# Infini-attention beside a top-1 mixture of experts: the last expert's second product as rows added into the output, and the last gathers, moved into the attention

## The chip, the cores and the metric

One core of a Trainium2 chip. Its engines run in parallel, each in its own order of instructions: TensorE (PE, matrix products), VectorE (DVE), ScalarE (ACT), GpSimd (POOL), and SyncE (SP), which here issues most DMAs; POOL issues the indirect ones. The metric is the device time of one execution in microseconds (us), smaller is better. The tables give the median of several runs and, apart from it, the one execution that the profiler recorded.

## The reference

`x` is 2048 x 512 in float32 (one batch). The output is a sum of three terms:

```
xn  = layernorm(x)
out = x + attention(xn) + moe(xn)

attention: q, k, v = xn@wq, xn@wk, xn@wv      32 heads of 16, four segments of 512 tokens
  per segment s: p = softmax(q k^T/4 + mask); a_dot = p v
                 a_mem = phi(q) M / (phi(q) z + 1e-6);  o = g*a_mem + (1-g)*a_dot
                 M += phi(k)^T v;  z += sum phi(k)          g = sigmoid(beta)
  result: o @ wo
moe: each token goes to the one expert with the largest logit of xn @ w_gate (8 experts)
  softmax over that single logit, so its weight is 1
  result: silu(xn @ w1[e]) @ w2[e]                512 -> 1376 -> 512
```

## The kernel before

**Precision and shapes.** Every float32 product of a weight is made of three float16 products: both operands are split into a high and a low half, and `mm3` (L406 to L409) adds high*high, low*high and high*low in one bank of the accumulator. The splits run on ACT, DVE and POOL (L388, L389 and L395 to L398). PE works in three shapes: full 128 x 128 tiles (projections, experts, `wo`), 64-row tiles (q times k, L1291) and 32-column tiles (probabilities times values, L1410).

**Stages.** The front computes layer norm, the q, k and v projections (their high and low halves are written by L785 and L786 and stored to `Q_d`, `K_d`), the memory terms (L791, L817, L823 to L826) and the routing. The routing sorts the experts by the number of their tokens, gives each rank a capacity (`CAPS`), and writes the lists of token indices by products of a one-hot `yT` (L690) with a table of selected values. The experts follow in that order: rows of `x` gathered (L1071), normalized and turned, the first product (`xgh, xgl` with `wh, wl`), silu (L1165, L1166, split into `hh, hl`), the second product. The second product has the weight tile as the stationary operand, so its result stands with features as partitions and tokens as columns; it is turned (L1175) and stored to the scratch tensor `ye_d` (L1185). Meanwhile the attention runs by units of heads: maxima (L1291 with a reduction on DVE, L1326), scores (L1291) with exp on ACT (L1383), a causal select on POOL (L1387), value products (L1410), normalization, and the output product `wo * oT`.

**The end.** For each of the 16 tiles of 128 tokens a row of `ye_d` is gathered by an indirect DMA on POOL (L1527), weighed on ACT (L1494), added to `x` on DVE (L1544), the output product is added on DVE (L1551), and the tile is stored to `out` (L1554). All 16 gathers need the last expert's rows in `ye_d`; the last tile of the output is made in two halves.

**What sets the order.** All instructions are recorded by a planner: each stage is a generator process with a key, and costs per instruction and due times (`QKV0`, `MOE0`, `ATT0`, `SLOT`, `PVA`, `OUT` and so on at the head of the file) decide which one PE and the other engines take next. On the chip each engine goes through its row of instructions in exactly that order and waits by semaphores for data.

## Time and profile before

| | us |
|---|---|
| median of 3 runs (lowest, highest) | 666.51 (663.81, 666.88) |
| the profiled execution | 669.71 |
| its span from first to last instruction | 667.8 |
| PE busy in the span | 639.8 (96%) |
| DVE, ACT, POOL busy | 546.1 (82%), 485.7 (73%), 383.8 (57%) |
| granted TensorE clock, mean | 0.984 |

The profiled execution lies 3.20 us above the median, and 1.9 us of it lie outside the span. Busy times are shares of the whole span; the rows below show single stretches.

### The profile page before, as it was taken

Reading aid. Unit: us, or ns where it says so; the run is one execution under the profiler, and the core shown is the slowest. Engines: PE = TensorE matmul, PEld = TensorE weight load, DVE = VectorE, ACT = ScalarE, POOL = GpSimd, SP = SyncE. Lnnn points to the kernel's source line nnn. Section 1 sums busy time; section 2 is a strip of 40 time slices with the busy share of each in tenths; the row PEclk is TensorE's granted clock in tenths of the full one; section 3 lists DMA queues with packets and bytes.
Section 4 is the critical chain, followed back from the end, with each engine's and each line's share of the span. In section 5 each row is a group of like instructions: output and inputs, shape, how many; then the busy total and the mean of one; then the engine's idle time right before and its main releaser. Section 6 shows DMA issues by size and latency. Waiting matters only on the chain.

```text
span 667.8 us, 17326 instructions
## 1 busy us (share of the span) xinstructions
PE 639.8 (96%) x5914; PEld 392.6 (59%) x5914; DVE 546.1 (82%) x1801; ACT 485.7 (73%) x1069; POOL 383.8 (57%) x596
## 2 busy tenths in 40 slices
PE   7999999999999899999999999989999999999965
PEld 5555555555675455656565566656566666677522
DVE  6875899844677999999998898999989989995435
ACT  5965475534561597999888688968778898899533
POOL 3510035001264487688768576876858786888770
PEclk9999999999999899999999999989999999999987
DMA  8813667435566557665584476564645666864485
GB/s 287 305 51 104 229 205 243 135 119 193 169 210 214 171 168 193 186 169 156 169 219 120 129 200 168 156 173 135 167 130 159 183 161 187 225 153 104 140 268 206
DMA packets 149054, 117.79 MB, mean 176 GB/s; under 512 B 34170, under 2 KB 136698, under 8 KB 148450
## 3 DMA queue, kind: packets, MB, share of 16 engines
q1 hardware_dynamic: 146290, 108.13, 54.9%
q0 software_dynamic: 2672, 8.52, 4.3%
q8 instruction: 47, 0.77, 0.5%
q14 instruction: 45, 0.37, 0.2%
HBM read 87.32 MB, written 29.30 MB: 175 GB/s over the span
## 4 chain that ended last, share of the span: by engine, by line
PE 71%; DVE 8%; ACT 7%; DMA 7%; issue 3%; another core or an unknown queue 2%; SPq 1%; POOL 1%; DVEq 0%; POOLq 0%; ACTq 0%
PE b L407 17%; PE b L409 15%; PE b L408 15%; PE b L1291 11%; PE b L1410 10%; DVE junk L1326 2%; DMA att<-in_A_x_dram 1%; PE b L817 1%; ACT pt L1383 1%; PE b L1098 1%; DMA K_d<-qkhl 1%; DMA Ks<-K_d 1%; DMA wh<-in_A_wk_dram 1%; DMA Qs<-Q_d 1%
## 5 line engine op out<-in xcount | busy, mean ns | idle before, releaser
L1326 DVE CUSTOM_DVE_ANT_0 junk<-b,mask 128x384 f16<-128x384 f32 (+3 forms) x512 | 218.7, 480 | 10.4 <-PE b L1291 9.3
L1383 ACT ACTIVATE pt<-b 128x512 f32<-128x512 f32 x320 | 173.1, 611 | 26.2 <-PE b L1291 25.8
L398 POOL TENSOR_TENSOR wl<-wst,wh 128x512 f16<-128x512 f32 (+3 forms) x120 | 119.1, 1004 | 50.3 <-ACT wh L396 44.0
L1387 POOL TENSOR_SCALAR_AFFINE_SELECT pt<-pt 128x256 f32<-128x256 f32 x256 | 111.0, 452 | 57.3 <-ACT pt L1383 55.8
L407 PE MATMUL b<-xgh,wh 128*128 128x288 f16 (+9 forms) x352 | 98.3, 279 | 0.9 <-DVE yb L1175 0.6
L407 PE MATMUL b<-hh,wh 128*128 128x288 f16 (+7 forms) x352 | 98.1, 279 | 0.3 <-DVE mxt L1326 0.2
L409 PE MATMUL b<-xgh,wl 128*128 128x288 f16 (+9 forms) x352 | 97.6, 277 | 0.0
L408 PE MATMUL b<-xgl,wh 128*128 128x288 f16 (+9 forms) x352 | 97.5, 277 | 0.0
L408 PE MATMUL b<-hl,wh 128*128 128x288 f16 (+7 forms) x352 | 97.4, 277 | 0.0
L409 PE MATMUL b<-hh,wl 128*128 128x288 f16 (+7 forms) x352 | 97.4, 277 | 0.0
L407 PEld LDWEIGHTS <-wh 128*128 128x128 f16 (+2 forms) x704 | 69.7, 99 | 39.2 <-issue 29.3
L398 POOL TENSOR_TENSOR hl<-yT,hh 128x288 f16<-128x288 f32 (+7 forms) x88 | 64.2, 731 | 36.1 <-ACT hh L396 35.5
L389 DVE SCALAR_TENSOR_TENSOR wl<-wst,wh 128x512 f16<-128x512 f32 (+2 forms) x96 | 74.1, 780 | 5.4 <-ACT wh L388 4.7
L1410 PE MATMUL b<-pt,vau 128*32 128x512 f32 (+3 forms) x1024 | 76.9, 436 | 0.7 <-ACT pt L1383 0.3
L395 ACT ACTIVATE wst<-wst 128x512 f32<-128x512 f32 (+3 forms) x120 | 63.9, 550 | 18.7 <-DVE mxt L1326 17.4
L409 PEld LDWEIGHTS <-wl 128*128 128x128 f16 (+2 forms) x704 | 69.9, 99 | 10.7 <-issue 0.2
L408 PEld LDWEIGHTS <-wh 128*128 128x128 f16 (+2 forms) x704 | 70.1, 100 | 9.9 <-issue 1.1
L1291 PE MATMUL b<-Ks,Qs 64*128 64x384 f16 (+3 forms) x512 | 64.5, 300 | 3.4 <-DVE mxt L1326 2.2
L388 ACT ACTIVATE wh<-wst 128x512 f16<-128x512 f32 (+2 forms) x96 | 54.8, 571 | 12.9 <-DMA wst<-in_B_w_dram 12.7
L396 ACT ACTIVATE wh<-wst 128x512 f16<-128x512 f32 (+3 forms) x120 | 61.4, 551 | 0.2
L1291 PE MATMUL b<-Qs,Ks 64*128 64x384 f16 (+3 forms) x512 | 61.4, 300 | 0.1
L1410 PEld LDWEIGHTS b<-pt,vau 128*32 128x32 f32 x1024 | 30.4, 109 | 46.5 <-issue 35.5
(209 smaller groups left out, 1192.2 us busy)
## 6 DMA issues: line engine op xcount, KB each, us to landing
wst<-in_B_w_dram SPq DMA_DIRECT2D x32, 640.0 KB
wst<-in_B_w_dram SPq DMA_DIRECT2D x24, 768.0 KB
Qs<-Q_d SPq DMA_DIRECT2D x64, 98.0 KB
Ks<-K_d SPq DMA_DIRECT2D x64, 98.0 KB
K_d<-qkhl SPq DMA_DIRECT2D x48, 128.0 KB
Q_d<-qkhl SPq DMA_DIRECT2D x48, 128.0 KB
vau<-V_d SPq DMA_DIRECT2D x16, 304.0 KB
V_d<-va SPq DMA_DIRECT2D x4, 1120.0 KB
```

Source lines behind the costliest of these rows:

```text
L389: yield vec(n, lambda: V.scalar_tensor_tensor(lo, src, scale, hi, op0=ALU.mult, op1=ALU.subtract), two=True)
L395: yield act(n, lambda: A.activation(src, src, AF.Copy, scale=scale), True)
L396: yield act(n, lambda: A.activation(hi, src, AF.Copy), True)
L398: yield gps(pool(n), lambda: G.tensor_sub(lo, src, hi))
L407: PE.matmul(outp, lh, rh, start=start, stop=False)
L408: PE.matmul(outp, lh, rl, start=False, stop=False)
L409: PE.matmul(outp, ll, rh, start=False, stop=stop)
L1291: PE.matmul(bs[a][:, off : off + w], lhs, rhs, start=True, stop=True)
L1326: yield vec(w, lambda: V.tensor_tensor_reduce(out=jk[:, :w], in0=b[:, off : off + w], in1=mask[:, L - w :], op0=ALU.add, op1=ALU.max, scal ...
L1383: yield act(L, lambda: A.activation(dst, src, AF.Exp))
L1387: yield gps(360, lambda: G.affine_select(dg, dg, pattern=[[0, 2], [1, P]], compare_op=ALU.is_ge, fill=0.0, base=0, channel_multiplier=-1))
L1410: PE.matmul(vb[32 * hh : 32 * hh + 32, j * P :], va[:, j, VW * h : VW * h + 32], ptt[u][0][:, hh // 2, hh % 2, POFF[j] : POFF[j] + w], sta ...
```

## The change

- The rank of the experts is changed: the sixth largest becomes the last, with capacity 256 (two row tiles of 128); the two smallest move one place forward.
- The last expert's second product has tokens as the stationary operand: for each of two row tiles, 11 chunks of the hidden dimension, three matmuls of 512 columns each. Its weights are loaded as whole rows of `w2`. All its weight splits stay on DVE (`VLAST`), and so does the low half of its silu (`ELAST`).
- These rows don't go to `ye_d`. When all tiles of `out` are stored, the last expert's rows are gathered from `out` (two indirect DMAs on POOL, L1264), the product is added on DVE (L1273), and they are scattered back (two indirect DMAs on POOL, L1275). For this a list of its tokens and gates (`tokl`, `gatel`) is made at the end of the routing by 16 one-hot tiles (L798) and 32 small products with 3 columns (L802); the planner lets expert 0's first product be recorded after that list.
- The 16 gathers from `ye_d` (now L1640) need seven experts and stand in the midst of the last attention units, in five buffers. The gather is added by four multiply-adds on DVE in place of the ACT pass and one add. Rows of `x` for late tiles go to buffers that are free earlier, each of the last four behind the store of the tile four before it.
- The first tiles of q and k (`Qs0`, `Ks0`) lie in a pool of their own, so that their loads and the first maxima no longer wait for the front's pool to be closed.
- The planner's constants are retuned.

```diff
-CAPS = (288, 288, 288, 270, 256, 256, 240, 224)
+CAPS = (288, 288, 288, 270, 256, 240, 224, 256)
...
+FST, SUMK, VLAST, ELAST = 83625.4532, 590731.4436, 56, 7
...
+        for t in range(NT):
+            rm = T(mp, (P, NL * P), F16, f"yT{t % 3}")
+            yield vec(NL * P, lambda: V.tensor_scalar(rm[:], ri[:, : NL * P], rankl[:, t, :], None, op0=ALU.is_equal))
+
+            def products():
+                for j in range(NL):
+                    PE.matmul(bl[:, j, :3], rm[:, j * P : (j + 1) * P], sell[:, t, :3],
+                              start=t == 0 and j == 0, stop=t == NT - 1 and j == NL - 1)
...
+        yield from chain(lists2)
+        banks.put(n, "M")
+        yield fl.settle()
+        listedl.up()
...
-        if share[0] >= 1.0:
+        if share[0] >= 1.0 and n < VLAST:
...
             yield prepped[e].wait()
+            if e == 0:
+                yield listedl.wait()
...
+            if e == E - 1:
+                iw = yield wst.get()
+                yb = T(mp, (P, 4 * 384), F32, f"wst{iw}")
+                for j in range(NL):
+                    fl.spawn(last_base(j, min(P, cap - j * P), yb[:, j * D : (j + 1) * D]), fl.cur.key + j)
+                for j in range(NL):
...
+                    for f, (fo, fw) in enumerate(FCH):
...
+                        yield pe(3 * 216, lambda: mm3(b[:w], hh[:fw, f, sl], hl[:fw, f, sl], h[:fw, f % 3, :],
+                                                      l[:fw, f % 3, :], f == 0, f == NF - 1))
+                    fl.spawn(last_rows(j, w, n, b, yb[:, j * D : (j + 1) * D]), fl.cur.key)
+                break
...
+    def last_base(j, w, yr):
+
+        yield summed.wait()
+        yield gps(1270, lambda: G.indirect_dma_start(
+            out=yr[:w], out_offset=None, in_=out,
+            in_offset=bass.IndirectOffsetOnAxis(ap=tokl[:w, j : j + 1], axis=0)), fl.software)
...
+    def last_rows(j, w, n, b, yr):
+
+        yield lastly.wait()
+        yield vec(D, lambda: V.scalar_tensor_tensor(yr[:w], b[:w], gatel[:w, j : j + 1], yr[:w], op0=ALU.mult, op1=ALU.add))
+        banks.put(n, "D")
+        yield gps(1100, lambda: G.indirect_dma_start(
+            out=out, out_offset=bass.IndirectOffsetOnAxis(ap=tokl[:w, j : j + 1], axis=0), in_=yr[:w], in_offset=None), SWD)
...
+        for t in range(LATE, NT):
+            i = t - LATE
+            if i < TPS:
+                att[t] = tiles[i]
+            else:
+                yield stored[i - TPS].wait()
...
+        tiles = T(mp, (P, NBLK[0] * P), F32, "yb")
+        tiles = [tiles[:, :D], tiles[:, D : 2 * D], T(mp, (P, D), F32, "yg")[:]]
+        tiles += [T(mp, (P, D), F32, nm)[:] for nm in ("xgn1", "yh")]
+        for t in range(NT):
+            i = yield yts.get()
             yield gps(1270, lambda: G.indirect_dma_start(
-                out=yt, out_offset=None, in_=ye_d[:],
-                in_offset=bass.IndirectOffsetOnAxis(ap=home_i[:, t : t + 1], axis=0)), SWE)
...
+            for q in range(4):
+                V.scalar_tensor_tensor(a[:, :, q, :], y[:, q], gates[:, t : t + 1], a[:, :, q, :], op0=ALU.mult, op1=ALU.add)
```

**The order on POOL near the end.** `pt` are the probabilities of an attention unit. Before, the gathers stand behind the last select:

```order
L398 TENSOR_TENSOR wl3_2201_10489<-wst1_2217_10607,wh3_2200_10488 96x128
L1387 AFFINE_SELECT pt0_2218_10664<-pt0_2218_10664 128x2x128 x7
L1441 TENSOR_TENSOR ot0_2156_10308<-ot0_2156_10308,omt0_2101_10039 128x32x16
L1387 AFFINE_SELECT pt1_2232_10771<-pt1_2232_10771 128x2x128 x8
L1527 DMA wh0_2251_10901<-ye_d_2_67,home_i_30_109 128x512
L1527 DMA wl0_2252_10902<-ye_d_2_67,home_i_30_109 128x512
L1527 DMA wh1_2253_10903<-ye_d_2_67,home_i_30_109 128x512
```

Now the last of the 16 stand between the selects of the last two units, and the new gather and scatter of `out` end the row:

```order
L1640 DMA yb_2223_10540<-ye_d_2_67,home_i_30_109 128x512
L1640 DMA yg_2224_10541<-ye_d_2_67,home_i_30_109 128x512
L1640 DMA xgn1_2225_10542<-ye_d_2_67,home_i_30_109 128x512
L1508 AFFINE_SELECT pt1_2231_10567<-pt1_2231_10567 128x2x128 x7
L1640 DMA yh_2226_10543<-ye_d_2_67,home_i_30_109 128x512
L1508 AFFINE_SELECT pt1_2231_10567<-pt1_2231_10567 128x2x128
L1562 TENSOR_TENSOR ot0_2135_10052<-ot0_2135_10052,omt0_2072_9762 128x32x16
L1640 DMA yb_2223_10540<-ye_d_2_67,home_i_30_109 128x512
L1264 DMA wst0_2268_10888<-out_0_dram,tokl_32_111 128x512 x2
L1275 DMA out_0_dram<-wst0_2268_10888,tokl_32_111 2048x512 x2
```

The gathers have moved ahead of the last selects, which now stand behind them on the same queue.

**The order on PE at expert 0's first product.** `xh, xl` with `whq, wlq` is a projection, `xgh, xgl` is expert 0's first product, `Mst` the memory product. Before, projections stand between pieces of expert 0:

```order
L407 LDWEIGHTS wh0_190_1211
L407 MATMUL b0_391_2440<-xgh_302_1938,wh0_190_1211 128x288
L408 LDWEIGHTS wh0_190_1211
L408 MATMUL b0_391_2440<-xgl_303_1939,wh0_190_1211 128x288
L409 LDWEIGHTS wl0_191_1212
L409 MATMUL b0_391_2440<-xgh_302_1938,wl0_191_1212 128x288
L407 LDWEIGHTS whq_44_129
L407 MATMUL b6_389_2421<-xh0_153_910,whq_44_129 128x512
L408 LDWEIGHTS whq_44_129
L408 MATMUL b6_389_2421<-xl0_154_911,whq_44_129 128x512
L409 LDWEIGHTS wlq_47_132
L409 MATMUL b6_389_2421<-xh0_153_910,wlq_47_132 128x512
```

Now all projections are done when expert 0 begins, and the last products of the list (`yT` one-hot) and of the memory stand directly ahead of it:

```order
L802 LDWEIGHTS yT0_427_2622
L802 MATMUL b4_332_2088<-hl_73_246,yT0_427_2622 128x3
L881 MATMUL b0_429_2627<-Mst3_58_143,phe2_423_2604 128x136 x2
L881 MATMUL b1_431_2647<-Mst3_58_143,phe2_423_2604 128x136 x2
L414 LDWEIGHTS wh0_198_1257
L414 MATMUL b6_435_2653<-xgh_319_2019,wh0_198_1257 128x288
```

Expert 0's first product has moved behind the list and the last memory products, where nothing else stands beside it.

**The order on DVE at the same place.** Before, the last projection's halves (`qkhl`, L786) and `phe` (L791) stand among the silus of expert 0 (`yT`, L1166):

```order
L1166 SCALAR_TENSOR_TENSOR yT2_420_2622<-yT2_420_2622,b6_418_2598 128x288
L786 SCALAR_TENSOR_TENSOR qkhl1_425_2653<-b0_414_2576,qkhl1_425_2653 128x512
L1166 SCALAR_TENSOR_TENSOR yT0_429_2673<-yT0_429_2673,b5_421_2623 128x288
L791 SCALAR_TENSOR_TENSOR phe0_426_2654<-phe0_426_2654,phr1_427_2655 128x512
L1166 SCALAR_TENSOR_TENSOR yT1_431_2692<-yT1_431_2692,b4_428_2672 128x288
L823 TENSOR_TENSOR dn10_434_2708<-b3_433_2695,e6_42_127 128x16
```

Now they stand among the one-hot tiles of the list (L798):

```order
L798 TENSOR_SCALAR yT0_421_2600<-hl_73_246 128x256
L890 TENSOR_TENSOR oms0_411_2554<-b5_418_2588,dn01_419_2591 128x256
L798 TENSOR_SCALAR yT1_425_2610<-hl_73_246 128x256
L798 TENSOR_SCALAR yT2_426_2617<-hl_73_246 128x256
L848 SCALAR_TENSOR_TENSOR qkhl1_422_2603<-b2_408_2532,qkhl1_422_2603 128x512
L798 TENSOR_SCALAR yT0_427_2622<-hl_73_246 128x256
L853 SCALAR_TENSOR_TENSOR phe2_423_2604<-phe2_423_2604,phr1_424_2605 128x512
L381 TENSOR_SCALAR gatel_33_112<-b4_332_2088 128x1
```

The one-hot tile of the list's last product has moved behind the halves of the last projection.

**The order on PE at the end.** Before, PE ends with the two 256-column halves of the output product's last tile:

```order
L408 LDWEIGHTS oTh1_2115_10132
L408 MATMUL b0_2288_11124<-wo_h_27_106,oTh1_2115_10132 128x256
L409 LDWEIGHTS oTl1_2116_10133
L409 MATMUL b0_2288_11124<-wo_h_27_106,oTl1_2116_10133 128x256
L1664 TENSOR_LOAD nb_i_40_120
```

Now it ends with 45 matmuls of the last expert's second product (`hh, hl` with `wh, wl`), behind the output products:

```order
L415 LDWEIGHTS hh_2207_10444
L415 MATMUL b6_2283_11097<-wh3_2274_10958,hh_2207_10444 128x512
L416 LDWEIGHTS hl_2208_10445
L416 MATMUL b6_2283_11097<-wh3_2274_10958,hl_2208_10445 128x512
L1772 TENSOR_LOAD nb_i_42_122
```

Between the last value product and these 45 there are 12 more matmuls of the same product and 48 of the output product (four tiles).

## Rows read from the trace of the kernel before

**Rows 1.** The page of the profile: busy time of each engine (share of the span, instructions), and the chain of work that ended last, by engine.

```profile
PE 639.8 (96%) x5914; PEld 392.6 (59%) x5914; DVE 546.1 (82%) x1801; ACT 485.7 (73%) x1069; POOL 383.8 (57%) x596
...
PE 71%; DVE 8%; ACT 7%; DMA 7%; issue 3%; another core or an unknown queue 2%; SPq 1%; POOL 1%; DVEq 0%; POOLq 0%; ACTq 0%
```

**Rows 2.** Stretches of the end (start:end in us, then the length, then busy us and instructions of PE, PEld, DVE, ACT and POOL, the granted TensorE clock, where 1.00 is 2.4 GHz, the DMA share and GB/s).

```profile
620.00:630.00 10.00, 9.60 (x104) 5.14 (x106) 3.59 (x7) 7.17 (x15) 6.68 (x16) 1.00 0.53 157
640.00:645.00 5.00, 3.97 (x19) 1.67 (x18) 1.05 (x2) 1.64 (x3) 3.78 (x5) 1.00 0.91 295
645.00:650.00 5.00, 1.38 (x4) 0.31 (x3) 0.00 (x0) 0.52 (x1) 3.78 (x5) 0.68 0.94 333
650.00:655.00 5.00, 3.80 (x9) 1.15 (x9) 2.92 (x5) 1.34 (x2) 0.13 (x1) 0.50 0.58 200
655.00:660.00 5.00, 5.00 (x27) 2.63 (x26) 4.64 (x9) 4.01 (x6) 0.00 (x0) 0.79 0.85 316
```

**Rows 3.** Timeline of PE in the last output products (start, duration as modelled, operation; in brackets the idle time before and what ended it).

```profile
630.63 0.39 PE L407 MATMUL b<-wo_h,oTh 128*128 128x512 f16 x1
...
643.38 0.38 PE L409 MATMUL b<-wo_h,oTl 128*128 128x512 f16 x1
643.59 0.38 PE L407 MATMUL b<-wo_h,oTh 128*128 128x512 f16 x1
645.68 0.38 PE L408 MATMUL b<-wo_l,oTh 128*128 128x512 f16 x1 [1.71 <-issue]
...
661.06 0.27 PE L409 MATMUL b<-wo_h,oTl 128*128 128x256 f16 x1
```

**Rows 4.** Timelines of POOL (first gather, the longest, the last), DVE (its longest wait and its last instructions) and SP (the last stores) at the end.

```profile
629.96 0.97 POOL L1527 DMA_INDIRECT wh<-ye_d,home_i  x1 [0.16 <-issue]
...
635.01 1.25 POOL L1527 DMA_INDIRECT wh<-ye_d,home_i  x1 [0.30 <-issue]
...
649.17 0.96 POOL L1527 DMA_INDIRECT wst<-ye_d,home_i  x1 [0.30 <-issue]
...
652.08 0.69 DVE L1551 SCALAR_TENSOR_TENSOR xg<-b,xg 128x512 f32<-128x512 f32 x1 [9.51 <-remote]
...
661.06 1.34 DVE L1551 SCALAR_TENSOR_TENSOR hl<-b,hl 128x512 f32<-128x512 f32 x3
...
661.77 2.15 SPq L1554 DMA_DIRECT2D out_dram<-hl  x3
```

**Rows 5.** Busy time of each engine in stretches of the start of the experts and of the attention, columns as in rows 2.

```profile
140.00:150.00 10.00, 10.00 (x83) 5.38 (x82) 3.94 (x12) 2.39 (x4) 0.47 (x1) 1.00 0.28 97
...
190.00:200.00 10.00, 8.53 (x72) 7.04 (x71) 8.03 (x15) 5.88 (x16) 7.51 (x11) 1.00 0.73 225
200.00:210.00 10.00, 9.28 (x78) 6.32 (x78) 6.49 (x20) 3.05 (x6) 7.87 (x12) 1.00 0.67 208
210.00:220.00 10.00, 8.49 (x58) 4.04 (x56) 10.00 (x49) 0.00 (x0) 0.00 (x0) 1.00 0.84 265
220.00:230.00 10.00, 8.85 (x57) 5.28 (x57) 9.76 (x39) 7.31 (x16) 5.94 (x6) 0.83 0.31 100
```

**Rows 6.** What PE waits for from 140 to 260 us: total, times, longest.

```profile
PE b L1291 <- DVE mxt L1326: 2.2, 3, 0.8
PE b L1098 <- DVE xgn L1089: 1.5, 1, 1.5
```

**Rows 7.** Groups of instructions of one shape: line, engine, operation, count, busy us, mean ns of one, idle time before.

```profile
L398 POOL TENSOR_TENSOR wl<-wst,wh 128x512 f16<-128x512 f32 x72 | 87.1, 1216 | 49.3 <-ACT wh L396 43.1 <-issue 5.7
...
L389 DVE SCALAR_TENSOR_TENSOR wl<-wst,wh 128x512 f16<-128x512 f32 x72 | 57.2, 796 | 4.8 <-ACT wh L388 4.1 <-POOL hl L398 0.5
...
L786 DVE SCALAR_TENSOR_TENSOR qkhl<-b,qkhl 128x512 f16<-128x512 f32 x32 | 21.8, 685 | 15.6 <-ACT qkhl L785 11.5 <-DMA wst<-in_B_w_dram 3.1 <-issue 0.7
...
L791 DVE SCALAR_TENSOR_TENSOR phe<-phe,phr 128x512 f32<-128x512 f32 x24 | 17.4, 724 | 0.0
...
L826 DVE TENSOR_TENSOR oms<-b,dn 128x256 f32<-128x256 f32 x24 | 10.1, 422 | 0.6
...
L690 DVE TENSOR_SCALAR yT<-hl,hh 128x288 f16<-128x288 f32 x16 | 7.6, 473 | 0.0
...
L825 DVE TENSOR_TENSOR dn<-dn,g_t 128x16 f32<-128x16 f32 x24 | 6.2, 259 | 0.7
...
L1544 DVE TENSOR_TENSOR att<-att,xgn 128x512 f32<-128x512 f32 x8 | 5.3, 687 | 1.8 <-issue 1.5 <-ACT xgn L1494 0.2
...
L1494 ACT ACTIVATE xgn<-wst,gates 128x512 f32<-128x512 f32 x6 | 4.0, 714 | 0.8 <-DVE att L1544 0.5
```

**Rows 8.** Timeline of PE where its shape changes from full tiles (L409) to 64-row tiles (L1291) and back; x4 counts concurrent or adjacent matmuls.

```profile
300.70 0.29 PE L408 MATMUL b<-xgl,wh 128*128 128x288 f16 x1
300.82 0.29 PE L409 MATMUL b<-xgh,wl 128*128 128x288 f16 x1
301.04 0.39 PE L1291 MATMUL b<-Qs,Ks 64*128 64x384 f16 x4
...
305.50 0.38 PE L1291 MATMUL b<-Ks,Qs 64*128 64x384 f16 x4
305.72 0.38 PE L1291 MATMUL b<-Qs,Ks 64*128 64x384 f16 x4
306.03 0.32 PE L407 MATMUL b<-xgh,wh 128*96 128x288 f16 x1
```

More of the change, by code (lines that the diff above doesn't have):

```diff
@@ L798, in project_out, with project_put @@
             es.put(ie)
-    def project_put(hl, i, dst, order):
+    def project_put(hl, i, dst, order, first):
         for r, h in enumerate(order):
@@ L804, in project_put @@
         hls.put(i)
+        if first:
+            laid_qk.up()
     def recall(s, c, pq):
@@ L1167, in silu @@
         banks.put(n, "D")
-        yield from split_pool(hh, hl, t, 1.0, cap)
+        yield from split_pool(hh, hl, t, 1.0, cap, there)
         yTs.put(i)
@@ L1247, in blank, with load, first_load @@
         cleared[i].up()
+    def load(u):
+        s, c = units[u // 2]
+        yield (scored[u - NH] if u >= NH else cleared[u]).wait()
+        for a in range(2):
+            for t, src in ((Qs[u % NH], Qd[s]), (Ks[u % NH], Kd[s])):
+                yield fl.dma(49 * 2048, 1024, lambda: SY.dma_start(
+                    t[64 * a : 64 * a + 3 * DH + 1],
+                    src[c].rearrange("(p a h) r t -> h a r p t", a=2, h=2)[u % 2, a]), 310)
+        loaded[u].up()
     def loads():
[L1251 to L1252 removed]
+        for u in range(1, 2 * NU):
             fl.cur.key = akey(u / 2, -LDA)
[L1254 to L1260 removed]
+            yield from load(u)
+    def first_load():
+        yield laid_qk.wait()
+        yield from load(0)
     MG = [((p, 3, 4 * P, 0),) if not r else ((p, 2, 3 * P, 0), (p, 0, P, 3 * P)) for p in range(2) for r in range(2)]
@@ L1497, in late_rows, with put_out @@
+        yield vec(D, lambda: V.scalar_tensor_tensor(att[t], b[:], 1.0 / WS, att[t], op0=ALU.mult, op1=ALU.add))
+        banks.put(n, "O")
+        attready[t].up()
+    def put_out(t):
+        yield fl.dma(P * D * 4, 2048, lambda: SY.dma_start(out[t * P : (t + 1) * P, :], att[t]))
+        yield fl.settle()
+        stored[t].up()
+        summed.up()
     def late_rows():
         yield prepared.wait()
-        xs = T(mp, (P, NG, D), F32, "xg")
-        late[:] = [xs[:, i, :] for i in range(NG)]
@@ L1502, in late_rows @@
-        order = [t for t in SUMS if t >= LATE]
-        for k, t in enumerate(order):
-            if k == NG:
-                yield spent.wait()
-                hs = [T(mp, (P, NF * CAP // 2), F32, nm) for nm in ("hh", "hl")]
-                late.extend(h[:, i * D : (i + 1) * D] for h in hs for i in range(3))
-            att[t] = late[k]
+        xg = T(mp, (P, NG, D), F32, "xg")
+        tiles = [xg[:, i, :] for i in range(NG)] + [T(mp, (P, D), F32, "xgn0")[:]]
+        for t in range(LATE, NT):
[4 more added lines that the diff above has]
+                yield stored[i - TPS].wait()
+                att[t] = T(oq, (P, D), F32, f"att{i - TPS}")[:]
@@ L1532, in sums @@
             fl.afresh()
[L1534 to L1555 removed]
+    yts = Slots(fl, 5)
@@ L1558, in overflow_table, with sum_out, add @@
+    def sum_out(t, yt, i):
+        yield fl.settle()
+        yield attready[t].wait()
+        def add():
+            a = att[t].rearrange("p (c q i) -> p c q i", q=4, i=BLK)
+            y = yt.rearrange("p (q c i) -> p q c i", q=4, i=BLK)
+            for q in range(4):
+                V.scalar_tensor_tensor(a[:, :, q, :], y[:, q], gates[:, t : t + 1], a[:, :, q, :], op0=ALU.mult, op1=ALU.add)
+        yield vec(740, add, two=True)
+        yts.put(i)
+        yield from put_out(t)
     def overflow_table(pool):
```

214 lines of the change are left out of this document (117 added, 97 removed).

## The prediction

> **What bounds the kernel now.** I read the page first, then the stretches of the end, then PE's timeline there, then the stretches around the start of the attention. The page says that PE is busy 96% of the span and is 71% of the chain that ended last [rows 1]. So an edit on another engine is worth what PE no longer waits, or what lies behind PE's last product. PE's work itself is the same in both programs: the columns of all its matmuls, at the pitch of .216 us for 512 that the output products keep (643.38 to 643.59 [rows 3]), come to 584 us before and after. Busy time is 639.8 us, so 56 us of it are changes of shape, slow clock and the like.
>
> PE loses time at two places. **The end:** from 630.63 to 661.33 (the last start and its .27) PE makes the last output products [rows 3]. They are 84 matmuls of 512 columns and 24 of 256: 84 x .216 + 24 x .108 = 20.7 us of work in 30.7 us. The loss of 10.0 begins at 643.59, with gaps before single matmuls that end on "issue", the first of 1.71 us [rows 3]; PE waits there for nothing that the profile shows, while the DMA share is .91 and .94, and the granted clock falls to .68 and then .50, its lower level of 1.2 GHz, right after those gaps [rows 2]. DVE's 9.51 us of waiting in that stretch is for these products [rows 4]. **The start of the attention:** in the 40 us from 190 to 230 PE is busy 8.53 + 9.28 + 8.49 + 8.85 = 35.15 us, and the clock is .83 in the last ten, worth 1.7 more [rows 5]: 6.5 us lost. The named waits are 2.2 us for the maxima on DVE and 1.5 for a normalized tile [rows 6]; DVE is busy 10.00 of 10 from 210 to 220 [rows 5], so a burst of maxima goes at DVE's pace.
>
> **The change part by part,** against the profiled 669.71.
>
> *The end of PE, -10.0.* Before, 16 gathers run back to back on POOL from 629.96 to 650.13 (the last starts at 649.17 and takes .96 [rows 4]), beside rows of x and stores of the output, while PE makes only output products. Now the gathers stand ahead of the last selects, and 22.7 us of PE work follow the last value product: 105 matmuls of 512 columns, the last 45 (9.7 us) with no gather from the scratch tensor beside them. I let the whole 10.0 go; between 0 and 10.0 is possible, since the cause of "issue" isn't shown. The clock's share goes with the gaps, because it fell after them.
>
> *A wait in the new end, +1.2.* The last piece of the expert's weights is loaded into a buffer that the add of tile 12 on DVE frees, and its splits stand behind the adds of tile 15. Two adds of about .687 give 1.4 [rows 7], nothing gives 0. I take 1.2, because PE reaches the piece right behind the output products.
>
> *Behind PE's last product, -1.0.* Before, 667.8 - 661.33 = 6.5 us: DVE's last adds, three stores whose issue ends at 661.77 + 2.15 = 663.92, and 3.9 more for the landing and the fixed end [rows 4]. Now one multiply-add of about .69, one scatter that I price as a gather, .96 [rows 4], and the same 3.9: 5.5. No scatter of this kind is in the trace; from .5 less to 2.5 more, so -1.5 to +1.5 in all. The gather of those rows waits for the store of tile 15, which by the same prices has landed and been read about 1 us before PE ends.
>
> *The start of the attention, -4.5.* The first q and k tiles load before the front is closed, and the first maxima stand 21 us of PE work earlier (162 instead of 183 in PE's columns), the first scores 6 earlier. The maxima ahead of the first scores are thus spread over 30.7 us of PE work instead of 16.3, and DVE need not run flat out to serve them. I take two thirds of the 6.5; 0 to 6.5 is possible, since a tile's normalization can still be late.
>
> *Changes of shape, +4.0.* Counted along PE's order, there are 319 changes between full, 64-row and 32-column matmuls before, 348 after. One from full to 64 rows costs 301.04 - 300.82 = .22 instead of the pitch of .12, so .10; one back .31 instead of .22 [rows 8]. If all of the 56 us were changes, one would be .175. 29 x .10 = 2.9 to 29 x .175 = 5.1; I take 4.0.
>
> *The list of the last expert, +4.0.* Before, PE has projections and expert 0 to choose from and is busy 10.00 of 10, while DVE is busy only 3.94 [rows 5]. Now all projections are over when expert 0 begins. The last one-hot tile of the list stands on DVE behind the halves of the last projection, and PE's last list and memory products stand ahead of expert 0. From the end of the last projection: three ACT passes of at most .714 (2.1), halves .685, one-hot .473, phi .724 [rows 7], and about .5 of small products: 4.5 us, with 1.5 of PE work beside it, so 3.0. If DVE comes late itself: in the last 9.4 us of PE's columns DVE has 14 one-hot tiles (6.6), 3 halves (2.1), 2 phi (1.4), 6 memory products (2.5) and 18 small operations of at most .26 (4.7), in all 17.3 us, 7.9 more than PE has [rows 7]. Below nothing it can't be, as PE had no gap there. I take 4.0, nearer to 3.0 because DVE was idle over half of that time before.
>
> *Hidden, 0.* Sixteen adds of .687 become four operations each on a quarter of the columns, at most the .422 of the row of 256 columns, so up to 16 x (1.69 - .69) = 16 us more; and 12 weight splits go from POOL (1.216) to DVE (.796, 9.6 us) [rows 7]. PE covers them: DVE is busy 3.59 of 10 from 620 to 630 [rows 2]. Without that cover it would be up to 26 us; the maxima, DVE's largest work, end earlier now, so I charge nothing. ACT loses 16 x .714, and is off the path.
>
> Sum: -10.0 + 1.2 - 1.0 - 4.5 + 4.0 + 4.0 = -6.3, so 663.4 for a profiled execution. That execution lies 3.2 above the median of 666.51, so **660.2** beside it.
>
> **The rivals.**
>
> *The gaps come again.* PE trickles in the new end as in the old. For it: "issue" isn't understood, and the gathers now run beside units in which DMAs run too. Against it: the first ten gathers, up to 643, left PE's pitch whole, and the gaps came only with a DMA share over .9 [rows 2, 3]. If half comes back with its clock, 5 to 8 us: 665 to 668, **666.4**, no measurable change.
>
> *The list costs more than the end gives (slower).* If DVE's backlog counts in full, PE stands 7.9 us before expert 0, and the clock falls after it as it fell at the end (.32 x 5 + .50 x 5 + .21 x 5 = 5.1 us there [rows 2]): 660.2 + 3.9 + 5.1 = 669.2; with the waits at the start unchanged, as the silus and maxima then queue behind the backlog, **673.7**. It decides from a hole of about 8 us on. Against it: DVE's idle time before, and that the one-hot tiles need nothing from PE but a free buffer.
>
> *POOL holds the selects (slower).* The 16 gathers stand (649.17 - 629.96) / 15 = 1.28 us apart, so 20.5 us of a queue in which selects stand behind them; 12 splits fewer give 14.6 back [rows 4, 7]. One gather took 1.25 instead of .96, beside adds on DVE [rows 4]; at .29 each, all 16 would add 4.6. With 20.5 - 14.6 + 4.6 = 10.5 us more before the last value products: **670.7**. It decides if a gather waits for a buffer that a late add frees. The Trainium skill, "SBUF — State Buffer", section "SBUF: two separate sides", speaks against this change here: GpSimd and some DVE operations share a port that one of them locks, and a DMA issued by GpSimd then waits for its descriptors. The row with 1.25 agrees with it. By that rule alone, without a blocked buffer, the change would cost up to the 4.6 us on POOL and give 660 to 665; by the rows of .97 and .96 it costs nothing, and I follow these, the first gather and the last.
>
> *More is gained.* DVE is early, the hole is nearly closed, and the start's loss goes wholly: -4.0 - 2.0, **654**.
>
> **How the numbers follow.** Forecast .53, more gained .13, gaps again .20, list .09, POOL .05. A measurement of this kernel can tell about 0.5% from no change: below 663.2 is faster, above 669.8 slower. So faster .66, same .20, slower .14. All low ends together give -10 - 6.5 + 2.9 - 1.5 = -15.1 (651.4), the high ends with the end's gain kept -10 + 5.1 + 7.9 + 1.4 + 1.5 = +5.9 (672.4). I leave out a tenth on each side: 650.5, for DVE's relief counted nowhere, to 669.0.
>
> **What would show it.** Right: PE's last 23 us at a pitch of .216, with clock 1.00; a gap of 3 to 5 us before expert 0's first product, put down to DVE; PE over 9.4 of 10 in every stretch of the first scores; 5 to 6 us behind PE's last matmul. Wrong: gaps with "issue" at the end or beside the moved gathers; POOL's gathers waiting for DVE with selects behind them; a hole of 8 us with a clock of .5 after it; or PE's chain ending in the last gather of `out` rather than in the products.

## The result, and the profile after

| | before | after |
|---|---|---|
| median of 18 runs each (lowest, highest), us | 666.50 (663.81, 669.20) | 669.07 (667.50, 676.27) |
| ratio after / before, 95% interval | | 1.0051 [1.0031, 1.0071] |
| the profiled execution and its span, us | 669.71, 667.8 | 668.49, 666.7 |
| start of PE's last matmul, us | 661.06 | 652.87 |

The change makes the kernel slower by half a per cent: the forecast was 660.2, and the sign is the other one. In the two profiled executions PE ends 8.2 us earlier, and yet the span is only 1.1 us shorter: what stands behind PE's last product grew from 6.5 to 13.5 us. And the profiled execution of before lies 3.2 us above its median, that of after .6 below its own.

Timelines of POOL, of DVE and of PE at the end of the changed kernel (L1264 gathers the last expert's rows from `out`, L1273 adds its product, L1275 scatters them back). They answer to [rows 3, 4]:

```profile
648.00 0.95 POOL L1264 DMA_INDIRECT wst<-out_dram,tokl  x1 [17.90 <-SPq L1773]
649.25 0.95 POOL L1264 DMA_INDIRECT wst<-out_dram,tokl  x1 [0.31 <-issue]
654.97 1.01 POOL L1275 DMA_INDIRECT out_dram<-wst,tokl  x1 [4.76 <-DVE wst L1273]
658.71 0.97 POOL L1275 DMA_INDIRECT out_dram<-wst,tokl  x1 [2.73 <-issue]
```

```profile
651.47 0.75 DVE L1273 SCALAR_TENSOR_TENSOR wst<-b,gatel,wst 128x512 f32<-128x512 f32 x1 [5.99 <-DMA wst<-out_dram,tokl]
654.21 0.75 DVE L1273 SCALAR_TENSOR_TENSOR wst<-b,gatel,wst 128x512 f32<-128x512 f32 x1 [2.00 <-DMA wst<-out_dram,tokl]
```

```profile
652.87 0.38 PE L416 MATMUL b<-wh,hl 96*128 96x512 f16 x1
```

The last product ends at 653.15. The second multiply-add still waits for the landing of its gather, the first scatter starts at 654.97 though its data stood ready at 652.22 (651.47 + .75), and the second starts 3.74 us behind the first. What POOL's sequencer does after the last scatter is in the views of the two source lines at the kernel's close (duration least/median/longest in ns, first and last start):

```profile
L1773 POOLq INC_SWDGE_SEM  x1: 980/980/980, 661.5 to 661.5; - x1
```

```profile
L1801 POOLq DRAIN  x3: 46/107/3328, 662.5 to 666.4; - x3
```

So behind PE stand 1.1 us of landing, .75 of the add, 3.7 from scatter to scatter, 2.7 more until the second has landed, 1.0 and 3.3 of POOL's closing, and .9: 13.5 us where 5.5 were forecast.

The stretches that answer to [rows 2, 5] (columns as there):

```profile
170.00:180.00 10.00, 7.06 (x53) 4.14 (x51) 7.75 (x26) 2.75 (x5) 0.00 (x0) 0.89 0.47 157
180.00:190.00 10.00, 9.52 (x63) 7.33 (x64) 4.34 (x20) 2.83 (x7) 2.55 (x5) 0.77 0.63 189
190.00:200.00 10.00, 10.00 (x81) 6.21 (x82) 9.83 (x38) 5.75 (x15) 6.99 (x11) 1.00 0.74 203
200.00:210.00 10.00, 8.52 (x75) 6.43 (x74) 10.00 (x37) 6.60 (x17) 6.50 (x9) 1.00 0.58 167
210.00:220.00 10.00, 10.00 (x90) 7.75 (x89) 10.00 (x31) 5.53 (x13) 7.39 (x7) 1.00 0.74 244
220.00:230.00 10.00, 10.00 (x85) 6.88 (x83) 9.97 (x39) 6.99 (x16) 4.13 (x7) 1.00 0.83 235
...
620.00:630.00 10.00, 8.37 (x53) 3.04 (x53) 10.00 (x24) 2.30 (x5) 9.67 (x11) 1.00 0.82 287
630.00:640.00 10.00, 9.53 (x45) 3.93 (x43) 9.17 (x19) 2.82 (x5) 0.10 (x1) 1.00 0.36 102
```

Three things are to be seen. From 190 to 230 PE is busy 38.52 of 40 us instead of 35.15 [rows 5], at full clock: the start of the attention is better, as forecast. From 170 to 190 there is a hole that before hasn't (10.00 of 10 there). And at 620, beside the moved gathers, where cover was assumed, DVE is now busy 10.00 and POOL 9.67, and PE 8.37. PE's own rows in the hole (q's last product, the list's L802, the memory's L881, expert 0's first):

```profile
174.23 0.38 PE L416 MATMUL b<-xh,wlq 128*128 128x512 f16 x1
...
175.60 0.20 PE L802 MATMUL b<-hl,yT 128*128 128x3 f16 x2 [0.50 <-DVE yT L798]
...
179.89 0.21 PE L802 MATMUL b<-hl,yT 128*128 128x3 f16 x2 [0.64 <-DVE yT L798]
180.58 2.15 PE L881 MATMUL b<-Mst,phe 128*128 128x136 f32 x8 [0.48 <-DVE gatel L381]
182.52 0.44 PE L414 MATMUL b<-xgh,wh 128*128 128x288 f16 x1
```

8.3 us lie between the starts at 174.23 and 182.52, with nothing but small products; PE then runs at .44 a matmul and not .29 until 184.4, at the lower clock. The named waits from 140 to 260 us, which answer to [rows 6], are few:

```profile
PE b L802 <- DVE yT L798: 2.9, 6, 0.6
PE b L414 <- DVE mxt L1447: 1.5, 1, 1.5
PE b L881 <- DVE gatel L381: 0.5, 1, 0.5
```

### The profile page after: what moved, and what is told of

The parts are those of the page before. It is cut to its first block, busy times and chain, and to the rows that moved or that the text cites. A ratio compares the mean times of both kernels' runs of the same rounds, so it can differ in the third digit from the quotient of the medians.

```text
span 666.7 us, 17255 instructions
## 1 busy us (share of the span) xinstructions
PE 639.3 (96%) x5868; PEld 384.4 (58%) x5868; DVE 562.9 (84%) x1911; ACT 469.8 (70%) x1033; POOL 370.6 (56%) x574
## 5 line engine op out<-in xcount | busy, mean ns | idle before, releaser
L414 PE MATMUL b<-xgh,wh 128*128 128x288 f16 (+8 forms) x352 | 98.3, 279 | 1.5 <-DVE mxt L1447 1.5
L415 PE MATMUL b<-xgl,wh 128*128 128x288 f16 (+8 forms) x352 | 97.5, 277 | 0.0
L416 PE MATMUL b<-xgh,wl 128*128 128x288 f16 (+8 forms) x352 | 97.5, 277 | 0.0
L414 PEld LDWEIGHTS <-wh 128*128 128x128 f16 x660 | 65.2, 99 | 41.7 <-issue 33.6
L414 PE MATMUL b<-hh,wh 128*128 128x288 f16 (+8 forms) x308 | 85.8, 279 | 0.2 <-DVE mxt L1447 0.2
L416 PE MATMUL b<-hh,wl 128*128 128x288 f16 (+8 forms) x308 | 85.0, 276 | 0.0
L415 PE MATMUL b<-hl,wh 128*128 128x288 f16 (+8 forms) x308 | 85.0, 276 | 0.0
L396 DVE SCALAR_TENSOR_TENSOR wl<-wst,wh 128x512 f16<-128x512 f32 (+3 forms) x106 | 76.7, 736 | 4.4 <-ACT wh L395 3.6
L415 PEld LDWEIGHTS <-wh 128*128 128x128 f16 x660 | 65.6, 99 | 10.2 <-issue 2.0
L416 PEld LDWEIGHTS <-wl 128*128 128x128 f16 x660 | 65.4, 99 | 9.9
L395 ACT ACTIVATE wh<-wst 128x512 f16<-128x512 f32 (+3 forms) x106 | 60.1, 578 | 8.9 <-DMA wst<-in_B_w_dram 8.9
L403 ACT ACTIVATE wh<-wst 128x512 f16<-128x512 f32 (+3 forms) x105 | 53.7, 545 | 0.0
```

Of the source, the lines that this page charges most:

```text
L395: yield act(n, lambda: A.activation(hi, src, AF.Copy, scale=scale), True)
L396: yield vec(n, lambda: V.scalar_tensor_tensor(lo, src, scale, hi, op0=ALU.mult, op1=ALU.subtract), two=True)
L414: PE.matmul(outp, lh, rh, start=start, stop=False)
L415: PE.matmul(outp, lh, rl, start=False, stop=False)
L416: PE.matmul(outp, ll, rh, start=False, stop=stop)
```

## The experiments

The theory after the result: the 10 us of gaps at the end of before belonged to that one execution; without them PE isn't what ends last, but the gathers, their weighing and the stores behind them. The change then moves PE's end little, and its own end, a chain of gather, add and scatter, costs what the moved gathers save. The rivals: the gaps were real and are saved, and the hole before expert 0 eats the gain; or the moved gathers hold up PE where they now stand.

| run | what it is | us median (range) | ratio to before, 95% | PE's last start, span |
|---|---|---|---|---|
| x0_before | before again | 666.47 (664.17, 671.18) | 1.0004 [.9975, 1.0033] | 650.54, 663.5 |
| x5_short | before, less PE work at the end | 667.19 (664.96, 670.11) | .9961 [.9930, .9991] | 640.45, 666.6 |
| x6_nogather | before without gathers | 659.12 (658.62, 660.05) | .9850 [.9808, .9892] | 652.85, 657.7 |
| x2_notail | after without its last chain | 657.88 (656.87, 663.00) | .9884 [.9850, .9919] | 653.92, 656.1 |
| x1_views | after, two views of `out` | 665.39 (663.84, 675.05) | .9978 [.9953, 1.0003] | 651.26, 661.7 |
| x9_notail2 | x2 again, with x7 | 662.39 (658.83, 666.30) | .9862 [.9815, .9909] | span 664.6 |
| x7_nolist | x2 without the list | 658.60 (657.66, 662.30) | .9819 [.9774, .9863] | span 660.6 |
| x3_list | list's workspace elsewhere | 680.95 (679.10, 682.45) | 1.0209 [1.0173, 1.0246] | span 679.6 |
| x4_pool | x1, one-hots on POOL | 672.04 (670.04, 678.12) | 1.0034 [1.0002, 1.0066] | span 670.8 |
| x8_split | x1, four one-hots on POOL | 671.63 (667.80, 676.16) | 1.0005 [.9973, 1.0036] | span 667.3 |
| x11_notail3 | x2 again, with x10 | 657.68 (656.60, 661.34) | .9889 [.9845, .9933] | 652.62, 654.8 |
| x10_nogather | x2 without the moved gathers | 652.97 (651.88, 654.55) | .9808 [.9772, .9844] | 647.97, 650.2 |

Each ratio is to runs of before on the same chip, whose medians were 666.66 (x0 to x3), 670.73 (x4 to x6), 670.93 (x7 to x9) and 666.42 (x10, x11).

**x0_before.** No edit: a second profile of the kernel before.

> The kernel before, once more, with a second profile. Theory A (the gap of some 10 us in the last output products belongs to every execution): its profile shows the idle time with 'issue' behind some 12 of the last output products again, 8 to 11 us between the first output product behind the last value product and PE's last one beyond the 20.7 us of work, and a profiled time near its median. Theory B (the profiled execution had more of it than the median one, 669.71 against 666.5): the gap is shorter here by 3 us or more, and the profiled time lies nearer 666.

Stretches of its end (columns as in [rows 2]), then pieces of its chain of waits in order of time (start, us, what):

```profile
640.00:645.00 5.00, 5.00 (x24) 2.25 (x23) 2.10 (x4) 2.17 (x3) 3.78 (x5) 1.00 0.91 284
645.00:650.00 5.00, 5.00 (x34) 3.13 (x33) 3.10 (x5) 2.44 (x4) 3.76 (x4) 1.00 1.03 389
650.00:655.00 5.00, 0.81 (x8) 0.48 (x5) 3.04 (x6) 2.62 (x4) 0.00 (x0) 0.84 1.03 390
655.00:660.00 5.00, 0.00 (x0) 0.00 (x0) 3.02 (x6) 0.72 (x1) 0.00 (x0) 0.50 0.62 232
```

```profile
648.43 6.72 DMA wst<-ye_d,home_i
...
655.23 0.73 ACT xgn L1494
...
657.79 0.74 DVE hl L1551 x2
```

PE's last matmul, and what POOL's sequencer does after its last gather (as for after above):

```profile
650.54 0.27 PE L409 MATMUL b<-wo_h,oTl 128*128 128x256 f16 x1
```

```profile
L1665 POOLq INC_SWDGE_SEM  x1: 904/904/904, 655.4 to 655.4; - x1
```

```profile
L1693 POOLq DRAIN  x3: 46/107/3000, 656.3 to 663.2; - x3
```

PE is busy without a gap until its last matmul starts at 650.54, 10.5 us earlier than in [rows 3], and the span is only 4.3 us shorter. It ends 12.7 us behind PE (663.5 - 650.8): the last gather takes 6.72 us from issue to landing while the DMA share is 1.03, then come the weighing, the adds and the last stores. So an end of PE that lies 10.5 us earlier goes with 4.3 us of span, not 10. Of the three profiles of this order with all gathers (before, x0 and x5 below) only the first has the gaps, so they don't belong to every execution; how often they come, three profiles can't tell.

**x5_short.** Before, with one of three matmuls in the output products of the last tiles, 13.8 us of PE work less:

```diff
+        if t >= LATE:
+            PE.matmul(b[:, cs], oh[:, k, sl], wo_h[:, k, cs], start=k == 0, stop=k == KD - 1)
+            return
```

> The kernel before with one instead of three matmuls per group in the output products of the last eight tiles (high times high alone, so these rows of the output are less exact): 13.8 us of PE work less, all of it behind the last value product; the order is otherwise the same. If the end of the kernel before is bound by the gathers and what follows them (landing, weighing, adds, stores), the time falls by under 2 us. If PE bounds it, as the prediction had it, the time falls by 8 us or more.

PE's last start is 10 us earlier than in x0, and the time falls by .4% (2.6 us), a little over the 2 us of the expectation's first branch and far from the 8 of its second: PE doesn't set the end of before. This profile's span goes on for 26 us behind PE's end.

**x6_nogather.** Before without the 16 gathers, their weighing and adding:

```diff
-            yield gps(1270, lambda: G.indirect_dma_start(
-                out=yt, out_offset=None, in_=ye_d[:],
-                in_offset=bass.IndirectOffsetOnAxis(ap=home_i[:, t : t + 1], axis=0)), SWE)
+            yield gps(1270, lambda: None, SWE)
```

> The kernel before without the 16 gathers, their weighing and their add (the experts' part is left out of the output); PE's order is the same. If the gathers bound the end, the end is PE's last product (650.8 in its second profile) and about 6 us behind it, so 656 to 659, 8 to 10 us below the kernel before. If PE bounds it, the time falls by under 2 us.

1.5% faster, with PE ending 2.3 us later than in x0 and the span 4.6 us behind PE's end. The gathered rows, with their weighing and adding, set the end of before: with x5, the theory stands for before. The rival that the gaps were saved falls for the medians, not for the one profiled execution that had them.

**x2_notail.** After, without the gather and scatter of the last expert; its product is still scaled, but added nowhere:

```diff
-        yield gps(1270, lambda: G.indirect_dma_start(
-            out=yr[:w], out_offset=None, in_=out,
-            in_offset=bass.IndirectOffsetOnAxis(ap=tokl[:w, j : j + 1], axis=0)), fl.software)
...
-        yield gps(1100, lambda: G.indirect_dma_start(
-            out=out, out_offset=bass.IndirectOffsetOnAxis(ap=tokl[:w, j : j + 1], axis=0), in_=yr[:w], in_offset=None), SWD)
```

> The changed kernel without the gather and the scatter of the last expert's rows (their product is made and scaled, but not added to the output, so the output lacks that expert). If the whole mechanism behind PE's last product costs what the trace shows beyond the 2 to 3 us that any end needs, the time is 10 to 11 us below the changed kernel, 658 to 659. By the prediction's own price of that end (5.5 us) it would be only 2 to 3 us below it, 666 to 667.

The median is 11.2 us below that of after, and the span ends 1.9 us behind PE. Without its last chain the change would have given 1.2%, more than the .9% forecast.

**x1_views.** After, with the two row tiles of the last expert gathered from and scattered to two views of `out` that are declared to be disjoint, so that the second pair doesn't wait for the first:

```diff
+    outs = dram_disjoint_views(out, NL)
...
-            out=yr[:w], out_offset=None, in_=out,
+            out=yr[:w], out_offset=None, in_=outs[j],
...
-            out=out, out_offset=bass.IndirectOffsetOnAxis(ap=tokl[:w, j : j + 1], axis=0), in_=yr[:w], in_offset=None), SWD)
+            out=outs[j], out_offset=bass.IndirectOffsetOnAxis(ap=tokl[:w, j : j + 1], axis=0), in_=yr[:w], in_offset=None), SWD)
```

> The changed kernel, with the gathers and scatters of the last expert's two row tiles through two views of the output that count as disjoint (the two lists name different tokens), so that the first scatter no longer waits for the second gather's landing and the second scatter no longer for the first one's; the order of instructions is the same on every engine. If the wait on the output tensor makes the long end (13.5 us behind PE's last product), the second scatter is issued about 4 us earlier, at PE's end plus 1.5, and the time falls by 3.5 to 4.5 us, to about 665. If the end is long because of the indirect DMAs themselves or of what closes the program, it falls by under 1 us.

POOL's timeline of its end:

```profile
646.39 0.95 POOL L1266 DMA_INDIRECT wst<-out_dram,tokl  x1 [17.91 <-SPq L1775]
647.64 0.95 POOL L1266 DMA_INDIRECT wst<-out_dram,tokl  x1 [0.31 <-issue]
650.82 1.01 POOL L1277 DMA_INDIRECT out_dram<-wst,tokl  x1 [2.22 <-DMA wst<-out_dram,tokl]
653.45 0.97 POOL L1277 DMA_INDIRECT out_dram<-wst,tokl  x1 [1.62 <-DVE wst L1275]
```

The first scatter starts .4 us before PE's last start, the second 2.63 us behind the first; the span ends 10.1 us behind PE instead of 13.5. So 3.4 us of the 13.5 were waits on the tensor `out`, and the medians differ by 3.7 (the ratios to before by .7%, some 5 us). The kernel is level with before, not faster: the chain and POOL's closing remain. No other run of the changed kernel with the whole output lies below before.

**x7_nolist and x9_notail2.** Of the same chip: x2 again, and x2 without the one-hot tiles and the list's products:

```diff
-            yield vec(NL * P, lambda: V.tensor_scalar(rm[:], ri[:, : NL * P], rankl[:, t, :], None, op0=ALU.is_equal))
+            yield vec(NL * P, lambda: None)
...
-                for j in range(NL):
-                    PE.matmul(bl[:, j, :3], rm[:, j * P : (j + 1) * P], sell[:, t, :3],
-                              start=t == 0 and j == 0, stop=t == NT - 1 and j == NL - 1)
+                pass
```

> The kernel without the gather and scatter of the last expert once more, on the same chip as x7, to compare with; 1.2% below the kernel before, as in its first run, if chips only scale the times.

> The kernel without the gather and scatter of the last expert (x2), and in addition without the 16 one-hot tiles on DVE and the 32 list products on PE (the list isn't made, the gates are ones; the order of the rest is the same). If these tiles on DVE are what holds PE ahead of expert 0, the idle time there falls from 6.5 us to 2.5 to 3.5 (the chain of the last projection: three ACT passes, halves, phi, memory product), the half clock behind it goes, and the time is 4 to 5.5 us below x2. If the last projection's own chain holds it, the time is within 2 us of x2.

The hole in x7, from q's last product to expert 0's first (PE's timeline):

```profile
172.67 0.38 PE L416 MATMUL b<-xh,wlq 128*128 128x512 f16 x1
...
179.00 0.45 PE L414 MATMUL b<-xgh,wh 128*128 128x288 f16 x1
```

The list is worth 3.8 us by the medians and .4% by the ratios, whose intervals overlap; that lies between the two branches of the expectation. The hole is 6.3 us instead of 8.3: three quarters of it aren't the list, but the last projection's own chain on ACT and DVE, with no other work for PE.

**x3_list.** The list works in another buffer, so that expert 0's first product can be recorded between the projections again:

```diff
+        lw = T(mp, (P, NBLK[0] * P), F32, "yb")
...
-            rm = T(mp, (P, NL * P), F16, f"yT{t % 3}")
+            rm = lms[t % 4]
```

> The changed kernel with the work space of the last expert's list moved out of the buffers of expert 0's hidden tiles (one copy of 128x256 more), so that expert 0's first product stands among the last projections and list products again. If the hole on PE before expert 0 (6.5 us idle and 1.1 us of half clock) is that order, PE is busy over 9.5 of 10 in each ten us from 160 to 190 and the time falls by 5 to 8 us, to 661 to 664. If PE's start of expert 0 only moves the wait to the attention's start (DVE is then late there), it falls by under 2 us.

Stretches of the hole, and one of the attention (columns as in [rows 2]):

```profile
170.00:180.00 10.00, 9.83 (x76) 6.27 (x73) 7.65 (x21) 6.58 (x16) 3.37 (x5) 1.00 0.50 154
180.00:190.00 10.00, 9.00 (x76) 6.14 (x77) 7.00 (x23) 4.01 (x10) 2.96 (x4) 1.00 0.45 136
...
220.00:230.00 10.00, 7.66 (x31) 4.10 (x31) 8.88 (x35) 2.35 (x6) 2.71 (x2) 0.51 0.52 156
```

The hole is mostly gone (1.2 us idle in these 20 instead of 3.4) and the clock stays whole, and the kernel is 2.1% slower: the planner, given the new place, records everything behind it in another order, and PE loses 4.2 us from 210 to 230 and 3.8 from 620 to 640, with a granted clock of .51 in the row of 220, near the lower of the two levels. The run shows that most of the hole can be filled; what filling it is worth alone it can't show, because the order changed with it. The expectation was missed.

**x4_pool and x8_split.** x1 with all 16 one-hot tiles on POOL, and with four of them there and a fourth buffer:

```diff
-            yield vec(NL * P, lambda: V.tensor_scalar(rm[:], ri[:, : NL * P], rankl[:, t, :], None, op0=ALU.is_equal))
+            yield vec(NL * P, lambda: G.tensor_scalar(rm[:], ri[:, : NL * P], rankl[:, t, :], None, op0=ALU.is_equal))
```

> The changed kernel with the two views of the output, and with the 16 one-hot tiles of the last expert's list made on POOL instead of DVE; the order of all other instructions on every engine is the same. POOL stands idle from 170 to 180 us there. If the hole on PE ahead of expert 0 is DVE's backlog, it shrinks from 6.5 us to about 3 (the halves and phi of the last projection stay on DVE), less half clock follows it, and the time falls by 3 to 5 us below the kernel with the views alone (665.4), to 660.5 to 662.5. If POOL's tiles are slower than DVE's by more than the backlog (over .7 us each against .35), PE waits for POOL instead and the time is the same or longer, 665 to 669.

> The changed kernel with the two views of the output, four instead of three buffers for the one-hot tiles, and four of the last eight tiles (8, 10, 12, 14) on POOL. If DVE's backlog in the 5 us ahead of expert 0 sets the hole, DVE has 4 x .35 = 1.4 us less there and PE starts expert 0 1 to 2 us earlier: 0.2 to 0.3% below the views alone, so 0.4 to 0.6% below the kernel before. If POOL's .92 us per tile is waited for, it is no faster than the views alone (0.2% below the kernel before) or slower.

Neither gains over x1. In x8 the hole is 7.8 us (173.30 to 181.10) where x1 has 8.3, a gain of .5 of the 1 to 2 us expected, and PE's last product still starts 5.0 us later than x1's: 2.0 of them are lost before 600 us and 3.0 from there to 636. The one-hot's group in x4, and then in x1 (count, busy us, mean ns, idle before):

```profile
L800 POOL TENSOR_SCALAR yT<-hl 128x256 f16<-128x256 f32 x16 | 15.1, 953 | 4.7 <-PE b L804 4.0 <-DVE dn L889 0.6
```

```profile
L800 DVE TENSOR_SCALAR yT<-hl 128x256 f16<-128x256 f32 x16 | 5.4, 340 | 0.0
```

POOL takes .95 us where DVE takes .34, so PE waits for POOL instead, and expert 0 begins at 182.60, 8.9 us behind q's last product. The Trainium skill, "GPSIMD Engine Reference", section "4.1 Engine selection", holds elementwise work with one input to be at roughly line rate there; here it is 2.8 times slower, and the measurement decides. x4's profile also has a stop that after's hasn't (PE's timeline):

```profile
611.01 0.37 PE L416 MATMUL b<-xgh,wh 128*128 128x256 f16 x1 [4.73 <-ACT pt L1506]
```

The same matmul of the order waits 4.92 us in x7 and 5.41 in x9, and not in the profiles of after, x1, x2, x8 and x11.

**x10_nogather and x11_notail3.** x2 without the 16 moved gathers and their adds, and x2 again on the same chip:

```diff
-            yield gps(1270, lambda: G.indirect_dma_start(
-                out=tiles[i], out_offset=None, in_=ye_d[:],
-                in_offset=bass.IndirectOffsetOnAxis(ap=home_i[:, t : t + 1], axis=0)), fl.software)
+            yield gps(1270, lambda: None, fl.software)
...
-        yield vec(740, add, two=True)
+        yield vec(740, lambda: None, two=True)
```

> The changed kernel without its last expert's gather and scatter, now also without the sixteen gathers of the first eight experts' rows and the additions of them to the output's rows: the output lacks all experts. If the moved gathers, which now run beside the seventh and the last expert's products, cost TensorE nothing, its last product starts where it did with them (653 to 655 us of the profile), and the time is that kernel's, within 0.5%. If they stop it by competing for the DMA engines (the stop of about 5 us near 605 us that some profiles showed), no stop of over 2 us stands between 600 and 620 us and the time is 3 to 6 us below. If gathered rows and their additions still bound the end, the time is 1 to 3 us below without any change between 600 and 620 us.

> The same kernel with the sixteen gathers and their additions kept (last expert's gather and scatter left out, so that the output lacks the last expert), on the same chip, to compare with: 0.984 to 0.989 of the time before. If the stop near 605 us comes by chance, this profile shows it or not without a change of code: it did in one of two profiles so far.

Stretches of x10, and its selects from 590 to 640 us as a group; behind them the same group of after:

```profile
610.00:620.00 10.00, 10.00 (x78) 5.23 (x76) 6.06 (x14) 4.53 (x11) 1.42 (x2) 1.00 0.79 268
620.00:630.00 10.00, 10.00 (x69) 4.33 (x68) 7.26 (x13) 1.96 (x5) 0.00 (x0) 1.00 0.40 143
```

```profile
L1503 POOL TENSOR_SCALAR_AFFINE_SELECT pt<-pt 128x256 f32<-128x256 f32 x16 | 7.0, 456 | 13.1 <-ACT pt L1499 13.1
```

```profile
L1508 POOL TENSOR_SCALAR_AFFINE_SELECT pt<-pt 128x256 f32<-128x256 f32 x16 | 10.2, 664 | 2.3 <-ACT pt L1504 2.3
```

PE's last product in x10, then in x11, and the wait of after's value products for selects from 590 to 640 us (total, times, longest):

```profile
647.97 0.38 PE L416 MATMUL b<-wh,hl 96*128 96x512 f16 x1
```

```profile
652.62 0.38 PE L416 MATMUL b<-wh,hl 96*128 96x512 f16 x1
```

```profile
PE b L1531 <- POOL pt L1508: 1.6, 2, 1.1
```

PE's last product starts 4.65 us earlier without gathers and adds, with no stop in either profile, and PE is busy 10.00 from 620 to 630 where after has 8.37 and x11 8.42. So the moved gathers with their adds cost PE 4.7 us where they now stand, or 5.5, as x10 still lay .85 us behind x11 at 600: the expectation that they cost nothing falls, and the stop isn't what they cost here. Of the 5.5 us, 3.6 arise from 618 to 628 us, at the last selects and value products, and 1.0 at the weight split of L396 that PE waits for near 645. The select takes .46 us without them and .66 beside them, and with the gathers ahead of it in POOL's row the last value products wait. The Trainium skill, "SBUF — State Buffer", section "SBUF: two separate sides", says that a DVE operation with two inputs in the SBUF and a GpSimd operation that reads the SBUF lock each other out of a shared port. The adds L1656 are such operations and the selects read the SBUF, so the slower selects agree with it; the run takes gathers and adds away together and can't tell which of the two slows them.

## Why the prediction was wrong

The step that failed is "The end of PE, -10.0", with the term behind it, "Behind PE's last product, -1.0". The first took the gaps of one execution for a property of the kernel, and the end of PE for the path that sets the time. One number stood against it before the result: that execution lay 3.20 us above the median. The prediction took these 3.2 us off its forecast and counted the gap as gained besides, so that what the gap had made of them was counted twice. x0, x5 and x6 show what bounds the end of before: the gathers' landing and the tiles behind them, 12.7 us after PE. The second term priced the new end by one scatter; the runs show 13.5 us for its 5.5, and the gather that was to have landed 1 us before PE's end landed 1 us behind it. Against the profiled execution, from which the sum starts, PE's end moved by -8.2 us where the sum has -5.3, and what stands behind it by +7.1 where it has -1.0: there the second term alone is the miss. Against x0, which lies near the median, the first term isn't there to be gained either. x2 gives the whole chain 11.2 us, x1 gives 3.4 to 3.7 of them to waits on `out` by span and median, and 4.3 (.98 + 3.33) are POOL's closing, which before has too (.90 + 3.00 in x0), but there it runs from 655.4 to 659.3 beside the last tiles' adds and stores.

The other terms, against x0's profile (665.29 us, near the median), by stretches, lost busy time and lost clock together:

| term | forecast | measured |
|---|---|---|
| start of the attention, 190 to 280 us | -4.5 | -7.7 (9.4 lost in x0, 1.7 in after) |
| list of the last expert, 140 to 190 us | +4.0 | +6.4 (3.4 idle, 3.0 of clock) |
| changes of shape | +4.0 | +4.1 (319 in x0 take 51.7 us beyond the pitch of their forms, 348 in after 55.8) |
| moved gathers, splits and adds hidden | 0 | +4.7 to 5.5 (x10), the next line included; +2.7 by the stretches from 590 us |
| wait in the new end | +1.2 | +1.2 (two waits of PE for L396's splits; part of the 2.7 above) |
| PE's end | | +2.3 (650.8 to 653.15) |
| behind PE's last product | -1.0 | +.8 (12.7 to 13.5) |

By the stretches, the rest of the program gives -3.5 more (-1.9 before 140 us, -1.6 from 280 to 590), so -7.7 + 6.4 + 4.1 + 2.7 - 3.5 = +2.0 of the 2.3 at PE's end. With the .8 behind PE the 2.3 make 3.1 us, where the medians differ by 2.6. The lines on the start of the attention and on the rest are read from two profiles; no run takes the retuned constants, the new rank or the pool of the first q and k tiles alone.

*Right:* the start of the attention in sign and place, and larger, though not by relief of DVE, which is busy 9.83 to 10.00 of 10 there in after: PE's waits for the maxima fall from 4.0 us in x0 to 1.7 (140 to 280 us); the changes of shape, by their own count (.16 us each; no row shows how the 584 us of columns behind the bound of .175 were counted); the wait for the late piece. *Mis-sized:* the list. Its hole is 8.3 us with a lower clock behind it, the size from which the rival "the list costs more" was to decide, and a sign of being wrong that the prediction had named; the backlog on DVE explains 2 us of it by x7, and the rest is the last projection's chain, beside which nothing was left for PE. *Wrong:* "Hidden, 0". The rival "POOL holds the selects" names the place of this cost; with 4.7 us for 10.5 it was half as large, and its gathers did wait for the add that frees a buffer, as it said (eight times in after, .3 to 1.2 us each). DVE's extra work was smaller than the bound (the adds take 20.1 us, 9 more than 16 of .687, not 16 more), and the cover failed all the same. The issue of the 16 gathers took 17.6 us, up to 1.96 for one, 2.3 more than 16 of .957: the prediction had left that at nothing. *The gaps come again:* in after's profile they don't; and x0 has none at a DMA share of .91 and 1.03, so the high share to which the prediction tied them doesn't make them by itself. What made them in before stays open. The stop of about 5 us that three of eight profiles of after's order show stands in the stretch of the moved gathers and may be why the runs of after reach 676, which no profile shows. All three come from the two chips on which before takes 670.73 and 670.93, where x8 has none; x10 had none in one profile, and neither had x11, so its cause stays open.

## What to carry to other kernels

Where one execution is profiled and lies above the median, profile it again before its gaps are counted as a gain; and ask by an experiment whether the engine that looks bound moves the end (here 13.8 us less PE work gave 2.6). A read-modify-write of the output at the very end is a chain of gather, add, scatter and the queue's closing, with nothing left to hide it: count every landing, the order that a shared tensor forces, and what the issuing engine does after its last DMA. Work moved into a stretch that was covered before is free only while the sum of what the covering engines do there still fits.

## What the runs showed of the hardware

- After its last indirect DMA POOL's sequencer takes .90 to .98 us for a semaphore increment and 3.00 to 3.33 us for a drain (x0, x1, after). It costs nothing while other engines still work, and the full 4.3 us where POOL ends last.
- A gather of 128 rows lands 6.72 us after its issue with a DMA share of 1.03 (x0), and two land 3.4 and 4.9 us after theirs with .40 and .30 (after); the 16 moved gathers of after take 3.6 to 8.4, with shares of .68 to 1.05 in their stretches. The scatters take 2.7 and 3.0. The Trainium skill, "DMA: Bandwidth & Descriptors", section "Latency and other measured facts", gives .2 us for the memory's latency on average and 2 us at high load, as the main part of a DMA's fixed cost. The direction agrees; against the page's difference of 1.8 us, the 6.72 us lie 1.8 and 3.3 above the two gathers of after, and queued transfers ahead may be in them.
- One kernel gave an execution with 10 us of gaps at PE's end (before) and one without (x0). The ends of their spans differ by 4.3 us only, because without the gaps another chain ends last.
